# Two attention and feed-forward layers on one core: a planner that keeps one queue of DMA transfers, and an order worked out anew

## The chip, the core and the metric

The kernel runs on one core of a Trainium2 chip. Five engines of the core follow their own instruction streams and meet through semaphores: PE (matrix products), ACT (ScalarE: exp, gelu, copies), DVE (VectorE: element-wise work, transposes of 32x32 blocks, statistics), POOL (GpSimd: masks, small powers) and SP, which here does nothing but issue DMA transfers, in order.

The metric is the device time of one execution in microseconds (us), as the median of several runs. Before the change it is 542.36 us (three runs, 541.82 to 544.45).

## What is computed

The input x has 2048 rows of 512 numbers (bf16). Two layers are applied, both with the same weights, and each layer is an attention block followed by a gated feed-forward block, both added to x:

```python
x = A_x
x = x + _A_ref(_layernorm(x), A_wq, A_wk, A_wv, A_wo, A_beta)
x = x + _B_ref(_layernorm(x), B_w_gate, B_w_up, B_w_down)
x = x + _A_ref(_layernorm(x), A_wq, A_wk, A_wv, A_wo, A_beta)
x = x + _B_ref(_layernorm(x), B_w_gate, B_w_up, B_w_down)

def _B_ref(x, w_gate, w_up, w_down):          # 512 -> 1792 -> 512
    return _gelu(x @ w_gate) * (x @ w_up) @ w_down

# _A_ref, per segment s of 512 rows, 32 heads of 16 numbers:
logits = einsum('bhqd,bhkd->bhqk', qs, ks) * scale + mask     # causal inside the segment
a_dot = softmax(logits) @ vs
pq = phi(qs)                                                  # phi(t) = t+1 if t > 0 else exp(t)
a_mem = (pq @ M) / (pq @ z + 1e-06)                           # memory of the segments before
o = g * a_mem + (1 - g) * a_dot
M = M + phi(ks)^T @ vs ;  z = z + sum(phi(ks))
```

A segment reads the memory that the earlier segments of its layer left, so the attention of segments 0 to 3 is a chain, while the scores of a segment, its projections and the feed-forward blocks depend only on their own rows.

## The kernel before

The work is cut into eight pieces k = 0 to 7: segment k % 4 of layer k // 4. For each k there is an attention part (class `Att`) and a feed-forward part (class `Ffn`). All of x, all weights and all intermediate results stay in on-chip memory; the weights are loaded once at the start, in pieces, in between the first work.

**One attention part.** The rows are normalised (`Norm`): DVE takes the statistics of each block of 128 rows (`bn_stats`, `bn_aggr`), POOL makes the factor (`scales`: `ve`, then `rs` by a power), DVE writes the normalised rows `xn` (`normed`, L738), and a transpose brings them into `xnT`: by a DMA transpose issued from SP (`turn_later`, L627), or by PE for those named in `BY_PE`. PE makes the projections q, k, v; each product is copied out of the accumulator banks (`evict`, L661 on DVE or L662 on ACT, whichever comes first in the plan). The scores of a step are made by 16- or 32-row matmuls that run side by side (a "visit", L1452), ACT takes exp of up to four banks in one instruction (`pt`, L1524, 128x2048), POOL zeroes what lies above the diagonal (L1497), and PE multiplies with the values (a "flush", L1148, which reads `vaug` and `vS`). DVE turns and divides the result (`byq`, `r`, `ab`, `aT`). For the memory, ACT and DVE make phi of the keys in a tile `e`, SP issues its transpose into `phik`, and PE sums it with the values (`upd_item`). The odd heads' keys go to `kB` and part of the values to `vS` by small DMAs.

**One feed-forward part.** After the output projection (`wo`) and the addition to x (L1249 on DVE) the rows are normalised again; 14 products with `wg_sb` (gate), 14 with `wu_sb` (up), and 4 with `wd_sb` (down, 14 matmuls each). Of the gate products the first `RAW` (8) are copied out as they are by DVE or ACT and get their gelu later in place (`gel<-gel`); the others get it straight from the accumulator bank (`gel<-big`, L1304). exp and gelu use different tables, so ACT reloads a table on each change between the two.

**PE's three ways of tiling.** A product runs as one matmul of 128x128 weights (L670) or as four of 128x32 weights side by side (L679), as `BY_COLUMNS` says by the number of the visit; both stream the same number of columns. Scores use tiles of 16 or 32 rows.

**What sets the order.** Nothing is scheduled at run time and nothing by hand: when the program is built, a planner (class `Clocks`, `Engine`, `Slots` and the loop at the end of the function) runs the kernel on clocks of its own. Each engine has a list of jobs with a cost in us and a slack; each PE item has a due time (`DUE`, `BIAS`, `DUE_STEP`), and numbers that change every 8 us of planned time (`CHANGES`). Whatever the planner takes next is emitted next, so its costs and due times fix the order of the instructions on all five engines, SP's too. Where no item is ready, the scores are not done and a bank is free, the planner emits a product that nobody reads (`warm`), here called a filler.

The planner's notion of DMA is coarse. A weight piece of `kb` KB pushes one clock, `ck.dma`; a transposed tile is taken to be there a fixed time after its issue, plus a margin (`MARGIN` 1.0, `PHI_MARGIN` 1.7), or 1.2 us after the weights queued so far; `kB` and `vS` are taken to be there 2.0 us after their issue plus `KB_MARGIN` 1.5:

```python
def dma_load(self, t, kb):
    self.dma = max(self.dma, t + 1.1) + kb / 200.0

def told(t2):                                             # in turn_later
    t3 = max(t2 + 1.4 + margin, ck.dma + 1.2)
    ck.at(t3 - 0.2, lambda: landed(t3))
```

Those clocks exist only in the planner. On the chip each consumer waits on the semaphore of its own transfer.

## Time and profile before

| what | value |
|---|---|
| median of three runs | 542.36 us (541.82 to 544.45) |
| the profiled execution | 542.17 us, of which the trace covers a span of 540.4 us |
| instructions in the trace | 20717 |
| PE busy | 524.6 us, 97% of the span |
| DVE busy | 434.4 us, 80% |
| ACT busy | 419.1 us, 78% |
| POOL busy | 239.3 us, 44% |
| granted PE clock | 1.00 throughout |
| DMA moved | 29.66 MB, mean 55 GB/s |

How to read it: the profile gives the busy time of each engine, cut into stretches of time (windows), groups of instructions by line, the waits (which engine sat idle, and what released it), a timeline, and for each kind of DMA the median time from issue to landing. A row such as "PE big L679 <- DMA phik<-e: 1.3, 2, 1.1" says that PE's instructions of line 679 that write `big` waited 1.3 us in total for transfers from `e` to `phik`, twice, the longest 1.1 us. PE's busy time counts overlapping matmuls once. `PEld` is the loading of weights into PE, which overlaps the matmuls.

### The profile page before, as it was taken

Reading aid. Unit: us, or ns where it says so; the run is one execution under the profiler, and the core shown is the slowest. Engines: PE = TensorE matmul, PEld = TensorE weight load, DVE = VectorE, ACT = ScalarE, POOL = GpSimd, SP = SyncE. Lnnn points to the kernel's source line nnn. Section 1 sums busy time; section 2 is a strip of 40 time slices with the busy share of each in tenths; the row PEclk is TensorE's granted clock in tenths of the full one; section 3 lists DMA queues with packets and bytes.
Section 4 is the critical chain, followed back from the end, with each engine's and each line's share of the span. In section 5 each row is a group of like instructions: output and inputs, shape, how many; then the busy total and the mean of one; then the engine's idle time right before and its main releaser. Section 6 shows DMA issues by size and latency. Waiting matters only on the chain.

```text
span 540.4 us, 20717 instructions
## 1 busy us (share of the span) xinstructions
PE 524.6 (97%) x9084; PEld 274.6 (51%) x9144; DVE 434.4 (80%) x844; ACT 419.1 (78%) x406; POOL 239.3 (44%) x417
## 2 busy tenths in 40 slices
PE   8989898999999999999999999999999999999997
PEld 4436464854445444444544444454444554445884
DVE  7997899999998998589985898788975979476162
ACT  6899887999999878988789778987879646972500
POOL 6558144664456355634383343833484343111000
PEclk9999999999999999999999999999999999999999
DMA  8628841304411321100342113313310043000001
GB/s 255 196 41 181 213 73 23 58 4 73 69 23 32 56 58 35 28 13 13 63 70 41 32 25 57 52 32 52 41 52 2 12 81 53 3 1 32 11 1 39
DMA packets 69483, 29.66 MB, mean 55 GB/s; under 512 B 55120, under 2 KB 68944, under 8 KB 69392
## 3 DMA queue, kind: packets, MB, share of 16 engines
q1 hardware_dynamic: 69248, 28.32, 25.8%
q8 instruction: 71, 1.16, 0.9%
q14 instruction: 20, 0.16, 0.1%
q10 hardware_dynamic: 144, 0.01, 0.0%
HBM read 9.71 MB, written 2.10 MB: 22 GB/s over the span
## 4 chain that ended last, share of the span: by engine, by line
PE 87%; DVE 6%; issue 3%; ACT 2%; DMA 2%; POOL 0%; SPq 0%; DVEq 0%; POOLq 0%; ACTq 0%
PE big L670 42%; PE big L679 29%; PE big L1452 8%; PE big L1148 6%; ACT pt L1524 1%; DMA phik<-e 1%; DVE x_sb L1249 1%; DVE st L702 1%; DVE byq L1176 1%; DMA x_sb<-in_A_x_dram 1%; DVE xn L738 0%; DVE ab L1184 0%; DVE aT L1191 0%; PE big L768 0%; ACT lost L1541 0%
## 5 line engine op out<-in xcount | busy, mean ns | idle before, releaser
L1524 ACT ACTIVATE pt<-big 128x2048 bf16<-128x2048 f32 (+1 forms) x151 | 272.8, 1811 | 71.2 <-PE big L1452 58.5
L1497 POOL TENSOR_SCALAR_AFFINE_SELECT pt<-pt 64x256 bf16<-64x256 bf16 (+3 forms) x300 | 155.7, 545 | 233.3 <-ACT pt L1524 232.2
L1339 DVE TENSOR_TENSOR gel<-gel,big 128x512 bf16<-128x512 bf16 x112 | 74.8, 681 | 35.6 <-PE big L670 22.2
L670 PE MATMUL big<-xnT,wg_sb 128*128 128x256 bf16 (+1 forms) x389 | 66.7, 321 | 1.2 <-issue 1.0
L1249 DVE TENSOR_TENSOR x_sb<-x_sb,big 128x512 bf16<-128x512 bf16 (+1 forms) x65 | 43.0, 668 | 20.8 <-PE big L670 14.6
L1176 DVE STREAM_TRANSPOSE byq<-big 128x512 f32<-128x512 f32 x64 | 44.9, 702 | 17.4 <-PE big L1148 9.2
L670 PE MATMUL big<-xnT,wu_sb 128*128 128x256 bf16 (+1 forms) x347 | 54.7, 311 | 0.8 <-issue 0.6
L670 PE MATMUL big<-wd_sb,gel 128*128 128x512 bf16 (+2 forms) x240 | 54.0, 367 | 1.4 <-issue 1.0
L670 PEld LDWEIGHTS <-wg_sb 128*128 128x128 bf16 x399 | 37.5, 98 | 24.2 <-issue 3.0
L679 PE MATMUL big<-wd_sb,gel 128*32 128x512 bf16 x824 | 49.3, 380 | 0.1
L679 PE MATMUL big<-xnT,wu_sb 128*32 128x512 bf16 x812 | 47.6, 379 | 0.0
L1148 PE MATMUL big<-pt,vaug 128*32 128x64 bf16 (+5 forms) x1152 | 44.7, 263 | 2.0 <-ACT pt L1524 1.8
L670 PEld LDWEIGHTS <-wu_sb 128*128 128x128 bf16 x357 | 33.9, 98 | 18.1 <-issue 1.9
L702 DVE BATCH_NORM_STATS2 st<-x_sb 128x6 f32<-128x512 bf16 x60 | 40.7, 678 | 0.3
L1304 ACT ACTIVATE gel<-big 128x512 bf16<-128x512 f32 x58 | 32.3, 603 | 8.1 <-PE big L670 8.0
L679 PE MATMUL big<-xnT,wg_sb 128*32 128x512 bf16 (+1 forms) x644 | 37.0, 372 | 0.0
L670 PEld LDWEIGHTS <-gel 128*128 128x128 bf16 x256 | 23.2, 98 | 26.0 <-issue 2.5
L1304 ACT ACTIVATE gel<-gel 128x512 bf16<-128x512 bf16 x54 | 31.0, 656 | 0.0
L679 PEld LDWEIGHTS <-wu_sb 128*32 128x32 bf16 x812 | 21.2, 97 | 19.1 <-issue 1.7
L679 PEld LDWEIGHTS <-gel 128*32 128x32 bf16 x824 | 21.0, 97 | 19.3 <-issue 2.0
L738 DVE TENSOR_SCALAR xn<-x_sb,mv,rs 128x512 bf16<-128x512 bf16 x62 | 27.9, 493 | 2.8 <-POOL rs L725 2.6
L843 POOL TENSOR_SCALAR kS<-kf,maskA 128x256 bf16<-128x256 bf16 x28 | 29.3, 1047 | 0.8
(124 smaller groups left out, 799.4 us busy)
## 6 DMA issues: line engine op xcount, KB each, us to landing
out_dram<-x_sb SPq DMA_DIRECT2D x15, 128.0 KB, 1.7
vS<-vaug SPq DMA_DIRECT2D x14, 136.0 KB, 2.7
wg_sb<-in_B_w_gate_dram SPq DMA_DIRECT2D x8, 224.0 KB, 5.4
kB<-kf SPq DMA_DIRECT2D x28, 64.0 KB, 2.5
wu_sb<-in_B_w_up_dram SPq DMA_DIRECT2D x8, 224.0 KB, 4.8
wd_sb<-in_B_w_down_dram SPq DMA_DIRECT2D x7, 256.0 KB, 6.3
x_sb<-in_A_x_dram SPq DMA_DIRECT2D x3, 512.0 KB, 6.1
xnT<-xn SPq DMA_TRANSPOSE x48, 2.5
```

What stands on the lines that cost most here:

```text
L670: nc.tensor.matmul(out, lhsT=lhsT, rhs=rhs, start=start, stop=stop)
L679: nc.tensor.matmul(out[r], lhsT=lhsT[:, r], rhs=rhs[c], start=start, stop=stop, tile_position=(0, 32 * c))
L702: nc.vector.bn_stats(out=self.st6[:, 0, :], in_=x_sb[:, self.tt0 + j, :])
L843: eng.tensor_scalar(out=kS[:, b, t, :, u], in0=self.kf[:, b, :].rearrange("p (t h c) -> p t h c", h=2, c=Q)[:, t, 0, :], scalar1=(maskA, m ...
L1148: nc.tensor.matmul(ps()[32 * j:32 * j + 32, q0 + shift:q1 + shift], lhsT=va[:, ki, values_of(va, b, p, j)], rhs=step["pt"][:, j, c0:c0 + q ...
L1176: nc.vector.transpose(out=self.byq[:, c], in_=ps()[:])
L1249: ck.dve.post(ck.made(), slack, (0.683 - 0.00104 * (D - width), lambda: nc.vector.tensor_tensor(out=xt, in0=xt, in1=ps()[:, 0:width], op=A ...
L1304: return lambda: nc.scalar.activation(out=out(), in_=in_(), func=ACT.Gelu_apprx_tanh)
L1339: ck.dve.post(ck.made(), NORMAL, (0.683, lambda: nc.vector.tensor_tensor(out=hidden(g, h), in0=hidden(g, h), in1=banked(ps), op=ALU.mult), ...
L1452: nc.tensor.matmul(big[:, got[j], c0:c0 + q1 - q0], lhsT=lhsT, rhs=a.q[rows, b, q0:q1], start=True, stop=True, tile_position=(32 * j, 0))
L1497: nc.gpsimd.affine_select(out=v, in_=v, pattern=[[0, m], [by, size]], compare_op=ALU.is_ge, fill=0.0, base=by - 1, channel_multiplier=-1)
L1524: 0.172 + 0.000832 * width * len(banks_of), lambda g=g, st=st: nc.scalar.activation(out=pt[:, g, 0:width], in_=st, func=ACT.Exp, scale=SCA ...
```

## The change

The two programs compute the same, with the same tiles. Changed are the planner's costs and all its fitted numbers, and with them the order of all instructions. By parts:

1. **One queue of transfers.** `ck.transfer(t, lag, service)` keeps one clock for all DMA: a transfer starts when it was issued plus its lag, or when the one before it ended, and holds the queue for its service time. Weight pieces take 1.55 us lag and kb/350 us, a transposed tile 0.05 and 1.2 us (after an issue of 1.3 us), a piece of `kB` 1.4 and 0.5 us, a piece of `vS` 1.55 and 0.5 us.
2. **Margins.** `MARGIN` 1.0 to 0.4, `PHI_MARGIN` 1.7 to 0.5, `KB_MARGIN` 1.5 to 0.4, `LANDING` 1.5 to 0.4, the extra time for `amT` 1.0 to 0.4.
3. **Costs of some engine jobs**: phi on ACT 1.06 to 0.93 and 0.632 to 0.55, its DVE part 0.775 to 0.70, the copies to `kS` on POOL 1.05 to 0.96, a change of PE's tiling 0.108 to 0.097.
4. **The first norm of segment 1 by halves**: its factors are made for two blocks of rows at a time (`cuts`), so POOL has two pairs of small instructions in place of one, and the first two blocks of rows need not await the statistics of the last two. Its statistics are posted from 12.0 us of planned time in steps of 0.3, in place of 12.9 and 0.5.
5. **All fitted numbers new**: due times, `BIAS`, `BY_COLUMNS` and 63 rows of `CHANGES` (`TUNING` stays); `RAW` 8 to 12 and `RAW_FIRST` 3 to 1.

```diff
-RAW_FIRST = 3
-HALF_DUE = 0.8949
+RAW_FIRST = 1
+HALF_DUE = 1.8596
...
-LANDING = 1.5
+LANDING = 0.4
 GELU_TILES = 1
-RAW = 8
...
+RAW = 12
...
-MARGIN = 1.0
-PHI_MARGIN = 1.7
-KB_MARGIN = 1.5
...
+MARGIN = 0.4
+PHI_MARGIN = 0.5
+KB_MARGIN = 0.4
...
-    **{("qk", k): d for k, d in {0: 0.2818, 1: 0.6658, 2: 3.2809, 3: 6.5204, 4: -2.3807, 5: -1.4922, 6: -0.9853, 7: -0.256}.items()},
...
+    **{("qk", k): d for k, d in {0: -0.5076, 1: 0.8217, 2: 1.6258, 3: 6.026, 4: -0.6428, 5: 0.7702, 6: 3.6216, 7: 1.9024}.items()},
...
-        self.dma, self.seen = 0.0, -1
+        self.dma, self.heavy, self.seen = 0.0, 0.0, -1
...
     def dma_load(self, t, kb):
 
-        self.dma = max(self.dma, t + 1.1) + kb / 200.0
+        self.heavy = self.transfer(t, 1.55, kb / 350.0)
+
+    def transfer(self, t, lag, service):
+
+        self.dma = max(self.dma, t + lag) + service
+        return self.dma
...
+    def arrives(t, landed):
+        ck.at(t - 0.2, lambda: landed(t))
+
     def turn_later(t, slack, out, in_, landed, margin=0.0):
 
         def told(t2):
-            t3 = max(t2 + 1.4 + margin, ck.dma + 1.2)
+            t3 = ck.transfer(t2, 0.05, 1.2) + margin
             ck.at(t3 - 0.2, lambda: landed(t3))
...
-            self.mv, self.rs, self.xnT, self.n, self.left = None, None, None, [0] * parts, [TPS // parts] * parts
+            self.cuts = 2 if key == ("xnTa", 1) else parts
+            self.mv, self.rs, self.xnT, self.n, self.left = None, None, None, [0] * self.cuts, [TPS // parts] * parts
...
-                part = j * self.parts // TPS
+                part = j * self.cuts // TPS
                 self.n[part] += 1
-                if self.n[part] == TPS // self.parts:
+                if self.n[part] == TPS // self.cuts:
                     self.scales(part, t)
...
-                        ck.sp.post(max(t, ck.pe), tn.KB_SLACK, (0.55, lambda r=r: nc.sync.dma_start(
-                            out=self.kB[r], in_=self.kf[r]), lambda t2: ck.at(t2 + 1.8, lambda: landed(t2 + 2.0))))
+                        ck.sp.post(max(t, ck.pe), tn.KB_SLACK, (0.62, lambda r=r: nc.sync.dma_start(
+                            out=self.kB[r], in_=self.kf[r]), lambda t2: arrives(ck.transfer(t2, 1.4, 0.5) + KB_MARGIN, landed)))
...
-            ck.act.post(max(ready, ck.pe), slack, (1.06, exp, lambda t: ck.dve.post(
+            ck.act.post(max(ready, ck.pe), slack, (0.93, exp, lambda t: ck.dve.post(
...
-    norm_of_input(1, 12.9, 0.5)
+    norm_of_input(1, 12.0, 0.3)
```

By kind, the built programs differ only in a few counts. PE has 9144 matmuls before and 9270 after. Of these, 96 and 84 are `warm` products (19 whole ones at the very start in both; then 19 groups of four and 1 whole one before, 12 groups of four and 17 whole ones after); the other differences come from products that run as one matmul or as four. PE changes its way of tiling 305 times before and 304 times after. On ACT 25 fewer gelus come from a 128x512 bank and 24 more are done in place, and the table loads are 18 in both; DVE has 25 more copies of 128x512 gate products. SP issues the same 198 transfers.

In the instruction order, names are the program's tiles, followed by the shape written; "x3" stands for three in a row.

SP's stream from its second pair of `phik` transposes (memory of segment 0) to the last weight piece; `wu_sb` and `wd_sb` are weights, `x_sb` is the load of rows of x. Before:

```order
L627 DMA_TRANSPOSE xnT<-xn 128x4x128
L515 DMA wu_sb<-in_B_w_up_dram 128x896
L515 DMA x_sb<-in_A_x_dram 128x4x512
L515 DMA wu_sb<-in_B_w_up_dram 128x896
L627 DMA_TRANSPOSE phik<-e 128x4x128 x2
L515 DMA wu_sb<-in_B_w_up_dram 128x896
L515 DMA wd_sb<-in_B_w_down_dram 128x2x512
```

And in the change:

```order
L635 DMA_TRANSPOSE phik<-e 128x4x128
L520 DMA wu_sb<-in_B_w_up_dram 128x896 x3
L520 DMA wd_sb<-in_B_w_down_dram 128x2x512
L520 DMA wu_sb<-in_B_w_up_dram 128x896 x5
L880 DMA kB_131<-kf 16x2048
L635 DMA_TRANSPOSE phik<-e 128x4x128
L880 DMA kB_131<-kf 16x2048 x3
L635 DMA_TRANSPOSE phik<-e 128x4x128 x2
```

The load of the last segment's rows of x no longer stands ahead of the transposes (it comes later), the weights come in one block, and the last two `phik` transposes of segment 0 stand behind that block and behind pieces of `kB`.

ACT's stream at the first exps (`vaug` are copies of v products, `e` is phi of keys). Before:

```order
L662 ACTIVATE vaug_132<-big 128x16x2x16 x2
L1524 ACTIVATE pt<-big 128x2048
L662 ACTIVATE vaug_132<-big 128x16x2x16 x2
L1524 ACTIVATE pt<-big 128x2048 x3
L973 ACTIVATE e<-kf 128x512 x2
L1524 ACTIVATE pt<-big 128x2048
```

And in the change:

```order
L670 ACTIVATE vaug_132<-big 128x16x2x16 x2
L1534 ACTIVATE pt<-big 128x2048
L670 ACTIVATE vaug_132<-big 128x16x2x16 x2
L1534 ACTIVATE pt<-big 128x2048
L983 ACTIVATE e<-kf 128x512
L1534 ACTIVATE pt<-big 128x2048
L670 ACTIVATE q<-big 128x512
```

Three exps stood in a row; now one `e` and then copies of q and k products stand between them. On PE, in the same place, the two visits that followed each other directly are apart, with 1 filler and 10 products of q and k between them, and 2 more products ahead of the flush that followed the visits at once before.

DVE's stream at the gate products of the fourth piece (k = 3). Before:

```order
L1176 STREAM_TRANSPOSE byq<-big 128x512
L738 TENSOR_SCALAR xn<-x_sb,mv,rs 128x512 x3
L1031 TENSOR_TENSOR am<-big,rdm 128x512
L661 CAST gel<-big 128x512
L984 TENSOR_SCALAR e<-e 128x512
```

And in the change:

```order
L669 CAST gel<-big 128x512 x2
L1186 STREAM_TRANSPOSE byq<-big 128x512
L669 CAST gel<-big 128x512 x7
L1186 STREAM_TRANSPOSE byq<-big 128x512
L1190 RECIPROCAL r<-byq 128x32
L1194 TENSOR_TENSOR ab<-byq,r 128x2x16x16
L1201 STREAM_TRANSPOSE aT<-ab 128x512
L669 CAST gel<-big 128x512
```

DVE copied 1 gate product there and now copies 10.

183 lines of the change are left out of this document (92 added, 91 removed).

## The prediction

> **What bounds the kernel now.** First the page's busy times, then its chain of work that ended last.
>
> ```profile
> span 540.4 us, 20717 instructions
> PE 524.6 (97%) x9084; PEld 274.6 (51%) x9144; DVE 434.4 (80%) x844; ACT 419.1 (78%) x406; POOL 239.3 (44%) x417
> PE 87%; DVE 6%; issue 3%; ACT 2%; DMA 2%; POOL 0%; SPq 0%; DVEq 0%; POOLq 0%; ACTq 0%
> ```
>
> PE is busy for 97% of the span and is 87% of the chain. A new order of the same products can gain two things only: PE's idle time and the products nobody reads. Where PE idles is in the windows (span of the window, then busy us and instructions of PE, PEld, DVE, ACT, POOL, the clock, and DMA):
>
> ```profile
> 20.00:40.00 20.00, 17.61 (x301) 8.31 (x302) 19.30 (x45) 19.34 (x20) 12.18 (x18) 1.00 0.28 55
> 40.00:60.00 20.00, 18.30 (x332) 11.88 (x334) 14.62 (x33) 18.57 (x22) 12.18 (x23) 1.00 0.89 193
> 60.00:80.00 20.00, 19.85 (x290) 11.79 (x293) 19.32 (x41) 18.16 (x17) 7.24 (x15) 1.00 0.53 119
> 80.00:100.00 20.00, 18.60 (x442) 10.64 (x436) 19.59 (x36) 15.29 (x10) 9.18 (x18) 1.00 0.28 38
> 100.00:540.00 440.00, 431.77 (x7623) 223.54 (x7664) 345.26 (x650) 333.91 (x321) 187.77 (x320) 1.00 0.20 36
> ```
>
> From 20 to 100 us PE idles 2.39 + 1.70 + 0.15 + 1.40 = 5.64 us; in all of the 440 us behind, 8.23 us, which is 0.37 per 20 us and spread thin. The waits of PE, for 20 to 100 us and then for 100 to 540 us, name the causes (total, times, longest):
>
> ```profile
> PE big L1148 <- ACT pt L1524: 1.8, 1, 1.8
> PE big L679 <- DMA phik<-e: 1.3, 2, 1.1
> PE big L1148 <- DVE x_sb L1249: 1.1, 1, 1.1
> PE big L670 <- issue: 0.3, 2, 0.2
> PE big L1452 <- ACT pt L1524: 0.3, 1, 0.3
> ...
> PE big L670 <- issue: 4.1, 26, 0.2
> PE big L670 <- DVE r L1180: 0.2, 1, 0.2
> ```
>
> Three causes, 1.8 + 0.3 for exps, 1.3 for the last transposes of the first memory update, 1.1 for an addition to x, make 4.5 of the 5.64 us. Behind 100 us PE waits for no other engine longer than 0.2 us at a time. So the old order is almost perfect there, and the change is decided in the first 100 us: between 4.5 and 5.6 us can be had there, and nothing behind it.
>
> **Fillers: a known loss.** The timeline (start, duration, instruction; in brackets idle before it and its releaser) shows a filler's price:
>
> ```profile
> 23.49 0.52 PE L1148 MATMUL big<-pt,vaug 128*32 128x256 bf16 x16
> 23.83 2.19 PE L679 MATMUL big<-warm 128*32 128x512 bf16 x36
> 25.96 0.29 PE L1452 MATMUL big<-q,kf 16*128 16x256 bf16 x4
> 26.19 0.39 PE L1452 MATMUL big<-q,kf 16*128 16x256 bf16 x8
> 28.40 0.51 PE L1148 MATMUL big<-pt,vaug 128*32 128x256 bf16 x16 [1.82 <-ACT pt L1524]
> ```
>
> 36 matmuls are 9 groups of four, and from their start to the next visit pass 2.13 us: 0.237 us each, a change of tiling included. Without the tail it is (2.19 - 0.38) / 8 = 0.226, 0.38 being one matmul's whole duration in the group below. I take 0.23. Behind the 19 of the start the order holds 20 fillers before and 29 after: 9 more, +2.1 us (2.0 to 2.1). They lie on PE, so nothing hides them.
>
> ```profile
> L679 PE MATMUL big<-warm 128*32 128x512 bf16 x76 | 4.9, 379 | 0.0
> ```
>
> The Trainium skill (TensorE: Matmul & The Clock Gate, Back-to-back issue gap) gives about 131 ns for each product of 512 columns in a sustained stream; by that page nine fillers would cost 1.2 us. The trace has 0.23 and decides.
>
> **The same products, otherwise.** More products of 256 columns run as four matmuls, 305 changes of tiling become 304, and there are 126 more matmuls by number but no more columns to stream, fillers aside. The price of a whole and of a fourfold product, from the groups with few records missing:
>
> ```profile
> L670 PE MATMUL big<-wd_sb,gel 128*128 128x512 bf16 x212 | 50.9, 379 | 1.4 <-issue 1.0
> L679 PE MATMUL big<-wd_sb,gel 128*32 128x512 bf16 x824 | 49.3, 380 | 0.1
> ```
>
> 50.9 / 212 = 0.240 and 49.3 / 206 = 0.239 us. I cost both edits at 0; a change of tiling more or less is bounded by the 0.2 to 0.4 us of one visit, either sign.
>
> **The exp wait (2.1 us).** In the timeline above two visits follow each other at 25.96 and 26.19, and the flush behind them waits 1.82 us, until 28.40, for the exp of the first. The new order puts 10 products and a filler between the visits and 2 more products before the flush, 13 x 0.23 = 3.0 us on PE, more than the wait. ACT has as many copies ahead of that exp as before, so the wait goes; bounds 0 to 2.1 gained, I take all. The halved norm of segment 1 helps these products to stand there. POOL's factor for four and for two blocks of rows:
>
> ```profile
> L725 POOL TENSOR_TENSOR rs<-ve,mhalf 128x4 f32<-128x4 f32 x13 | 13.5, 1041 | 1.1
> L719 POOL TENSOR_SCALAR ve<-mv 128x4 f32<-128x4 f32 x13 | 3.0, 230 | 7.3 <-DVE mv L711 6.5 <-POOL pt L1497 0.2
> L725 POOL TENSOR_TENSOR rs<-ve,mhalf 128x2 f32<-128x2 f32 x4 | 2.9, 715 | 0.3
> ```
>
> The first two blocks have theirs after 0.23 + 0.72 = 0.95 us in place of 1.27, and need not await the last two statistics. The second pair is 0.63 us more on POOL, 2 x 0.95 - 1.27, beside the 7.8 us that POOL idles in 20 to 40 us; without that cover it would be 0.6 us.
>
> **The phik wait (1.3 us).** Of the transposes of `phik`, first all in the run, then those between 48 and 60 us; and DVE's two steps of a half phi of q:
>
> ```profile
> DMA to landing us min/median/max: 2.4/2.4/7.2
> ...
> L627 SPq DMA_TRANSPOSE phik<-e x2: 1202/1263/1324, 49.7 to 51.0; - x2
> DMA to landing us min/median/max: 6.2/6.7/7.2
> ...
> L957 DVE SCALAR_TENSOR_TENSOR phiq<-q,phiq 128x1024 bf16<-128x1024 bf16 x12 | 16.9, 1411 | 0.4
> L953 DVE TENSOR_SCALAR phiq<-phiq 128x1024 bf16<-128x1024 bf16 x12 | 5.9, 493 | 1.6 <-ACT phiq L950 1.6
> ```
>
> These two took 6.2 and 7.2 us in place of 2.4, since weights and rows of x were queued ahead of them. The old planner did not know, the new one does. But the last two transposes now stand behind nine weight pieces and pieces of `kB`, and the `e` of the last has on DVE two such phi of q ahead of it, 2 x (0.49 + 1.41) = 3.8 us, that came later before. What was late by the queue is then late by DVE. Bounds: 0 to 1.3 us left; I leave 0.7.
>
> **The wait for x (1.1 us).** A flush finds its bank only when DVE has added an earlier one to x; DVE is busy 19.59 of 20 us there. The new order makes DVE's work in that stretch no less. Bounds 0 to 1.1; I leave 0.4.
>
> **Smaller margins.** Medians from issue to landing, and the planner's own sums:
>
> ```profile
> vS<-vaug SPq DMA_DIRECT2D x14, 136.0 KB, 2.7
> kB<-kf SPq DMA_DIRECT2D x28, 64.0 KB, 2.5
> xnT<-xn SPq DMA_TRANSPOSE x48, 2.5
> ```
>
> For `xnT` the planner allowed 1.3 + 1.4 + 1.0 = 3.7 us from the start of the issue and now 1.3 + 0.05 + 1.2 + 0.4 = 2.95; for `phik` 4.4 and 3.05; for `kB` 4.05 and 2.92; for `vS` 4.05 and 3.15. All still lie 0.4 to 0.65 us above the median, so a lone transfer isn't late. What is new is small slips where a chain runs later than planned: 0 to 1.5 us, I take 0.4.
>
> **Gate copies on DVE.** By shape:
>
> ```profile
> L661 DVE CAST gel<-big 128x512 bf16<-128x512 f32 x31 | 21.1, 685 | 4.4 <-PE big L670 2.2 <-PE big L679 1.7 <-PE big L1452 0.2
> L1304 ACT ACTIVATE gel<-big 128x512 bf16<-128x512 f32 x58 | 32.3, 603 | 8.1 <-PE big L670 8.0
> L1304 ACT ACTIVATE gel<-gel 128x512 bf16<-128x512 bf16 x54 | 31.0, 656 | 0.0
> ```
>
> 25 more copies at 0.685 are +17.1 us on DVE; on ACT 25 x 0.603 leave and 24 x 0.656 come, +0.7. DVE's 434.4 become 451.5, 84% of the span: hidden behind PE on average, but not everywhere (below). On the path I take 0.
>
> **Sum.** Stalls removed: 5.1 (between 4.5 and 5.6), less what is left or new, 0.7 + 0.4 + 0.4 = 1.5, is 3.6. Against the profiled execution's 542.17 us: 542.17 + 2.1 - 3.6 = 540.7. That execution stands 0.2 below the median of 542.36, so I forecast 540.9 us, 0.27% faster. About 0.5%, 2.7 us, is what a measurement of this kernel can tell from no change; the forecast lies inside.
>
> **Rivals.**
>
> *All stalls go.* If the one queue is right in every place, 542.36 + 2.1 - 5.6 = 538.9. For it: the three waits are what a coarse DMA clock and a coarse start would miss. Against it: DVE, busy 96% and more of 20 to 40 and of 60 to 100 us, has to keep up with a PE that runs earlier.
>
> *The waits move only.* The last `e` and the addition to x are as late as before, and only the exp wait goes: 542.36 + 2.1 - 2.1 = 542.4. The change would then have repaired in its plan what the chip has for another reason.
>
> *DVE becomes the bound.* From 60 to 200 us:
>
> ```profile
> 60.00:200.00 140.00, 136.60 (x2717) 74.49 (x2732) 131.89 (x256) 123.96 (x113) 71.89 (x118) 1.00 0.29 54
> DVE gel L1339 <- PE big L679: 1.8, 1, 1.8
> DVE x_sb L1249 <- PE big L679: 1.2, 2, 0.7
> ```
>
> DVE has 8.1 us left of 140, and its two longest waits are 1.8 and 1.2 us. The second and third gate blocks fall there; the order gives them 17 copies on DVE where 9 stood, 8 x 0.685 = 5.5 us. If DVE can't take more than half of that in its gaps, PE waits for free banks for 2.8 us, and the early gain is lost at the same engine but for the exp: 542.36 + 2.1 - 2.1 + 2.8 = 545.2. It decides once DVE's work up to 200 us grows by more than about 3 us, its two waits. Against it: what DVE does for other parts may move out of the stretch, and banks let PE run ahead. The Trainium skill (TensorEngine Tiling (Array Packing), PSUM Bottleneck) warns that when PE is made faster the copying out of banks may be the limit, and to use both ScalarE and VectorE for it; the change shifts copies towards VectorE, and the trace's 131.89 of 140 says that the warning is near.
>
> *Margins too small.* At each of the six boundaries between pieces behind 100 us a transposed row comes late by the 0.75 us that `xnT` lost: 6 x 0.75 = 4.5 and 542.36 - 1.5 + 4.5 = 545.4. For it: nothing there waits now, so there is only loss to have. Against it: medians below the plan in all four kinds.
>
> **How the numbers follow.** Forecast 0.42, all stalls gone 0.24, waits move 0.19, DVE the bound 0.09, margins 0.06. Faster by over 0.5% (below 539.65) are all stalls gone and 0.04 of the forecast's lower edge, 0.28; slower (above 545.07) are the last two but for 0.02 that stay just under, 0.13; within, 0.59. The forecast's own range is 539.4 to 542.4 (stalls left 0 to 3.0). The range for 8 in 10 reaches from 537.9, the 538.9 of all stalls gone less 1.0 of the thin idle, to 545.0, just under the two slower cases.
>
> **What would show it.** PE's idle time in 20 to 100 us falls from 5.64 to about 2 us, and PE's rows of `warm` rise by 9 products. No wait of a flush for `pt` over 0.5 us before 40 us. Transposes of `phik` in 45 to 60 us land in 2.4 to 4 us. DVE's busy time rises to about 451 us; if PE waits for DVE between 100 and 200 us by more than 1 us in total, the DVE rival holds. Idle of PE behind 100 us above 10 us in place of 8.23 would prove the margins. The forecast is wrong if early idle stays above 4 us or falls below 0.5.

## The result: slower by 0.9%

| | median | runs |
|---|---|---|
| before | 542.36 us | 541.82 to 544.45 |
| after | 547.90 us | 546.94 to 548.98 |

The ratio is 1.0093, with a 95% interval of 1.0068 to 1.0118. The forecast was 540.9 us; the range ended at 545.0. The profiled execution of the changed kernel took 548.07 us with a span of 546.3, which is 5.9 more than the 540.4 of before. That execution has a mean granted clock of 0.997 (3.4 us at half speed lower the mean of such a span by 0.003); the other four of the changed kernel have 1.000 and are as long, 546.94 to 548.98 us, so what its trace shows of a slow clock is not what they lost.

The page of the changed kernel, its span, busy times and the shares of the chain that ended last:

```profile
span 546.3 us, 21016 instructions
PE 528.2 (97%) x9210; PEld 276.7 (51%) x9270; DVE 446.7 (82%) x869; ACT 416.8 (76%) x402; POOL 238.5 (44%) x423
PE 74%; DVE 12%; ACT 6%; DMA 3%; issue 3%; SPq 1%; POOL 0%; ACTq 0%; DVEq 0%
```

PE is busy 97% again, but only 74% of the chain lies on it, 87% before. The windows of the same stretches (columns as before):

```profile
20.00:40.00 20.00, 19.09 (x342) 8.91 (x341) 18.76 (x47) 19.52 (x21) 11.10 (x20) 1.00 0.55 113
40.00:60.00 20.00, 16.98 (x277) 11.46 (x274) 15.43 (x34) 19.07 (x21) 13.97 (x20) 1.00 0.72 180
60.00:80.00 20.00, 19.58 (x449) 13.02 (x452) 15.79 (x34) 14.14 (x15) 3.88 (x10) 0.91 0.27 62
80.00:100.00 20.00, 19.49 (x454) 11.16 (x458) 18.74 (x44) 19.22 (x22) 11.76 (x26) 1.00 0.30 56
100.00:540.00 440.00, 431.25 (x7537) 221.62 (x7577) 360.24 (x671) 331.32 (x307) 185.38 (x320) 1.00 0.20 36
```

PE idles 0.91 us from 20 to 40 us in place of 2.39, but 3.02 from 40 to 60 in place of 1.70, and from 60 to 80 us the granted clock is 0.91. PE's waits, first from 20 to 100 us, then from 100 us on:

```profile
PE big L687 <- DMA phik<-e: 2.2, 1, 2.2
PE big L1462 <- ACT pt L1534: 1.7, 3, 0.9
PE big L678 <- issue: 0.3, 2, 0.2
...
PE big L678 <- issue: 3.5, 22, 0.2
PE big L1462 <- ACT pt L1534: 1.0, 2, 0.5
PE big L687 <- issue: 0.6, 1, 0.6
PE big L1462 <- issue: 0.5, 1, 0.5
PE big L687 <- DMA xnT<-xn: 0.4, 1, 0.4
```

The long exp wait of a flush (1.8 us) and the wait for x (1.1) are gone, as forecast. The wait for `phik` has grown from 1.3 to 2.2, and waits for exps, for `xnT` and for nothing named have come behind 100 us.

**A ledger.** Busy and idle time do not tell the loss, since the products nobody reads (fillers below) count as busy, and a slow clock too. So I summed, from PE's weight loads in the trace, the time beyond what the needed products take when the clock is granted in full: 0.216 us for 512 columns, start to start, plus the median of a change of tiling (0.32 us for a visit, 0.11 for the others). What is left is lost: fillers, idle time, half clock. In us, up to a point of the span, and the same for the plan's own clock:

| lost up to | 20 | 30 | 50 | 65 | 100 | 115 | 540 us |
|---|---|---|---|---|---|---|---|
| before, on the chip | 7.4 | 13.3 | 13.9 | 15.5 | 17.0 | 17.1 | 18.4 |
| before, in its plan | 7.1 | | 14.4 | 14.4 | 15.4 | 15.5 | 18.5 |
| after, on the chip | 7.5 | 10.6 | 14.1 | 17.8 | 18.6 | 21.1 | 24.2 |
| after, in its plan | 7.1 | | 13.9 | 13.9 | 14.0 | 16.4 | 16.2 |

The last column explains the result for the two profiled executions: 24.2 - 18.4 = 5.8 of the 5.9 us. The old plan foresaw its loss to 0.1 us (its clock ends at 537.4, and PE's last weight load in the trace starts at 537.3), but in part by luck: at 115 us the chip was 1.6 us behind it, and behind 115 us it lost 1.3 us where the plan has 3.0. The new plan promised 2.1 us less (its clock ends at 535.3) and the chip lost 8 us more than it promised. At 30 us the new order is 2.7 us ahead; at 50 us nothing is left of it, neither on the chip nor in the plan. Then come three losses: 50 to 65 us, 100 to 115 us (this one planned), and behind 115 us. Each is tried below.

**What the plan's promise consists of.** The new planner counts a change of PE's tiling at 0.097 us in place of 0.108: 305 x 0.108 = 32.9 us before, 304 x 0.097 = 29.5 after. That is 3.4 us less for almost the same changes, more than the whole promise of 2.1; at the old cost the same order would end at 538.7 in its plan (535.3 + 304 x 0.011), behind the old one. The trace does not bear the lower cost out: a visit with its two changes takes 0.32 + 0.11 = 0.43 us in it, and the planners count 0.226 for a visit of the smallest kind and two changes, 0.44 before and 0.42 after. This is also why the row of the new plan falls from 16.4 to 16.2 us behind 115 us, which a loss that is only added to can't do. Held against the same prices, the new plan holds no gain on PE.

### The profile page after: what moved, and what is told of

Read it like the earlier page. It is cut to its first block, busy times and chain, and to the rows that moved or that the text cites. A ratio compares the mean times of both kernels' runs of the same rounds, so it can differ in the third digit from the quotient of the medians.

```text
span 546.3 us, 21016 instructions
## 1 busy us (share of the span) xinstructions
PE 528.2 (97%) x9210; PEld 276.7 (51%) x9270; DVE 446.7 (82%) x869; ACT 416.8 (76%) x402; POOL 238.5 (44%) x423
## 3 DMA queue, kind: packets, MB, share of 16 engines
q8 instruction: 72, 1.18, 0.9%
## 4 chain that ended last, share of the span: by engine, by line
PE 74%; DVE 12%; ACT 6%; DMA 3%; issue 3%; SPq 1%; POOL 0%; ACTq 0%; DVEq 0%
PE big L678 36%; PE big L687 25%; PE big L1462 7%; PE big L1158 6%; ACT pt L1534 3%; DVE gel L1349 1%; DVE st L711 1%; DMA xnT<-xn 1%; DVE phiq L967 1%; DVE byq L1186 1%; DMA phik<-e 1%; DVE gel L669 1%; DVE xn L747 1%; DMA wu_sb<-in_B_w_up_dram 1%; SPq L520 1%
## 5 line engine op out<-in xcount | busy, mean ns | idle before, releaser
L1507 POOL TENSOR_SCALAR_AFFINE_SELECT pt<-pt 64x256 bf16<-64x256 bf16 (+4 forms) x304 | 151.2, 524 | 237.5 <-ACT pt L1534 222.6
L678 PE MATMUL big<-xnT,wg_sb 128*128 128x512 bf16 (+1 forms) x366 | 66.1, 329 | 1.6 <-issue 0.6
L687 PE MATMUL big<-xnT,wu_sb 128*32 128x512 bf16 (+1 forms) x1100 | 56.9, 358 | 0.0
L1186 DVE STREAM_TRANSPOSE byq<-big 128x512 f32<-128x512 f32 x64 | 45.1, 706 | 10.6 <-PE big L1158 10.1
L678 PE MATMUL big<-xnT,wu_sb 128*128 128x256 bf16 (+1 forms) x276 | 47.3, 320 | 1.1 <-issue 0.6
L669 DVE CAST gel<-big 128x512 bf16<-128x512 f32 x54 | 36.3, 683 | 10.6 <-PE big L678 5.2
L687 PEld LDWEIGHTS <-wu_sb 128*32 128x32 bf16 x1100 | 30.4, 99 | 20.6 <-issue 1.7
L1314 ACT ACTIVATE gel<-gel 128x512 bf16<-128x512 bf16 x74 | 39.7, 623 | 0.0
L678 PEld LDWEIGHTS <-wu_sb 128*128 128x128 bf16 x285 | 26.8, 98 | 17.1 <-issue 1.9
L852 POOL TENSOR_SCALAR kS<-kf,maskB 128x256 bf16<-128x256 bf16 x28 | 30.5, 1090 | 0.4
L1462 PE MATMUL big<-q,kf 16*128 16x64 bf16 (+5 forms) x576 | 27.7, 263 | 2.0 <-ACT pt L1534 1.8
```

What stands on the lines that cost most here:

```text
L669: ck.dve.post(ck.made(), slack, (cost, lambda: nc.vector.tensor_copy(out=dst(), in_=src()), end), taken=taken)
L678: nc.tensor.matmul(out, lhsT=lhsT, rhs=rhs, start=start, stop=stop)
L687: nc.tensor.matmul(out[r], lhsT=lhsT[:, r], rhs=rhs[c], start=start, stop=stop, tile_position=(0, 32 * c))
L852: eng.tensor_scalar(out=kS[:, b, t, :, u], in0=self.kf[:, b, :].rearrange("p (t h c) -> p t h c", h=2, c=Q)[:, t, 0, :], scalar1=(maskA, m ...
L1186: nc.vector.transpose(out=self.byq[:, c], in_=ps()[:])
L1462: nc.tensor.matmul(big[:, got[j], c0:c0 + q1 - q0], lhsT=lhsT, rhs=a.q[rows, b, q0:q1], start=True, stop=True, tile_position=(32 * j, 0))
```

## Experiments

In all kernels but those named as planned anew, the edit is made where instructions are issued, with the planner's clocks untouched, so that all other instructions keep their order. Ratios are to the kernel before.

### 1. Without the fillers

```diff
-                product(ps()[:], warm[:], wide)
+                (only the planner's counters, as product() moves them)
                 ck.unread(Clocks.MM[512])
```

The changed kernel without its 29, the kernel before without its 20:

> The changed kernel without the 29 products that nobody reads, their places in the plan kept, so every other instruction stands in the same order. If they lie on PE, as I costed them, the time falls by 29 x 0.216 = 6.3 us, from 547.9 to 541.6. If they only fill time in which PE would wait for banks and exps anyway, idle time takes their place and the time stays between 546.5 and 548.

> The kernel before without its 20 products that nobody reads, all else in the same order. On PE: 20 x 0.216 = 4.3 us less, 538.1. Only filling waits: 541.5 to 542.5. The difference between this fall and that of the changed kernel is what the 9 additional ones cost: 2.0 us by the first theory, 0 by the second.

Measured: the kernel before 543.02 us, ratio 1.0001 (0.9993 to 1.0010): no gain. The changed kernel 544.36, 1.0040 (1.0024 to 1.0056): 3.5 us less than the 547.9 with them. For the kernel before without fillers, PE's waits from 20 to 100 us, and then two rows of PE's timeline:

```profile
PE big L1452 <- ACT pt L1524: 3.1, 3, 1.9
PE big L1148 <- ACT pt L1524: 1.8, 1, 1.8
```

```profile
25.75 0.29 PE L1452 MATMUL big<-q,kf 16*128 16x256 bf16 x4 [1.93 <-ACT pt L1524]
28.18 0.83 PE L1148 MATMUL big<-pt,vaug 128*32 128x256 bf16 x16 [1.81 <-ACT pt L1524]
```

Where nine fillers stood, PE now waits 1.93 us for the same exp, and the visit starts at 25.75 in place of 25.96. The windows of the same run show what is worse:

```profile
26.00:34.00 8.00, 6.18 (x85) 2.34 (x77) 6.30 (x17) 7.54 (x7) 4.76 (x7) 0.57 0.13 27
```

After two idle stretches of 1.93 and 1.81 us the clock stands at half for most of 8 us. So in the kernel before the fillers cost nothing: they stand where PE would wait, and they keep the clock up. For the changed kernel the time alone does not say so, since it fell by 3.5 us, of the 6.3 that the fillers would cost on PE. By the ledger both orders have lost about the same at 50 us with fillers (13.9 and 14.1) and without (15.1 and 15.1). So up to there the fillers are not what is lost, and the 3.5 us come later. In the two profiled executions PE comes 1.3 us later to the `phik` products and the transpose is there, so the wait and the half clock of experiment 2 don't happen (3.2 us gained from 55 to 65 us), and three stalls of 0.5 to 0.6 us between 250 and 310 us are gone, for a reason that I did not find.

### 2. The wait for phik

SP's timeline of the changed kernel, and PE's:

```profile
49.68 1.45 SPq L880 DMA_DIRECT2D kB<-kf  x1
51.23 2.46 SPq L635 DMA_TRANSPOSE phik<-e  x1
53.76 1.84 SPq L880 DMA_DIRECT2D kB<-kf  x3
55.70 1.23 SPq L635 DMA_TRANSPOSE phik<-e  x1
...
57.77 0.24 PE L687 MATMUL big<-vaug,phik 128*32 128x32 bf16 x12
60.20 0.60 PE L687 MATMUL big<-vaug,phik 128*32 128x32 bf16 x52 [2.18 <-DMA phik<-e]
60.61 2.75 PE L687 MATMUL big<-xnT,wu_sb 128*32 128x256 bf16 x48
```

and DVE's, for the `e` of the last transpose:

```profile
53.06 0.76 DVE L986 SCALAR_TENSOR_TENSOR e<-kf,e 128x512 bf16<-128x512 bf16 x1
```

The `e` is done at 53.8; the plan had it at 54.4. DVE is early, not late. But SP, behind nine weight pieces and a slow transpose (2.46 us to issue), begins three pieces of `kB` only at 53.76, where the plan had finished them at 53.2. The transpose goes out at 55.70 and lands 4.45 us later. The plan had it issued from 54.4 on and there at 57.0, and at 57.5 with its margin: of the 3.1 us that it lands late, 1.3 are SP's and 1.9 the longer way from issue to landing. The second price is in the windows behind the wait:

```profile
60.00:61.00 1.00, 0.80 (x61) 0.74 (x64) 0.06 (x1) 0.23 (x1) 0.00 (x0) 0.61 0.00 0
61.00:62.00 1.00, 1.00 (x26) 0.85 (x20) 0.63 (x1) 0.00 (x0) 0.00 (x0) 0.50 0.00 0
62.00:63.00 1.00, 1.00 (x28) 0.74 (x20) 0.38 (x1) 0.00 (x0) 0.00 (x0) 0.50 0.06 16
63.00:64.00 1.00, 1.00 (x26) 0.55 (x19) 0.62 (x3) 0.04 (x1) 0.00 (x0) 0.68 0.00 0
```

PE's clock is granted at half for 3.4 us: the 48 matmuls at 60.61 take 2.75 us, and 1.50 in the next kernel. Two edits take the transpose out of the queue, in the changed kernel and, the first, in the kernel before:

```diff
 a_wu_early, b_wu_early: the eight loads of wu issued together
+  ahead of the first piece of wd (26 us) in the changed kernel,
+  ahead of the first transpose of phik (27 us) in the kernel before
 a_kb_act: the four pieces of kB of segment 1
-  nc.sync.dma_start(out=self.kB[r], in_=self.kf[r])
+  nc.scalar.dma_start(out=self.kB[r], in_=self.kf[r])
```

> The changed kernel with its eight pieces of wu issued at about 26 us, where SP is idle, in place of 45 to 50 us; nothing else moves. If the weight pieces ahead of them on SP and in the DMA engines make the last transpose of phik late, it is issued at about 53.8 (its e is ready then) in place of 55.7 and lands by 58.2: PE's wait of 2.2 us goes, and with it the half clock behind it, about 1.4 us: 544.3. If DVE sets it, as I predicted (e late), or if another thing is late next, the idle at 58 us only shrinks by some tenths: 547 to 547.9.

> The changed kernel with the four pieces of kB of segment 1 issued by ACT in place of SP. If SP's order is what makes the last phik transpose late (three pieces of kB, 1.84 us, stand between its e and its issue), it goes out at 53.8 and the wait and the half clock go: 544.5. If the transfers themselves are slow (weights in the DMA engines), the landing stays near 60 and the time at 547.5 to 548; if ACT's four issues delay its exps, 548 or more.

> The kernel before with its eight pieces of wu issued at about 27 us, where SP is idle until 35, in place of 45 to 57 us. In the changed kernel the same edit brought the last phik transposes in by 58.1 and let PE run 2.9 us earlier at 65 us, of which 1.1 were left at the end. Theory: here the 1.65 us that PE loses at 55 us go, and since the plan behind has its old margins nothing gives them back: 542.4 - 1.6 = 540.8, which beats both kernels. Rival: the gain is eaten by the next late thing (the addition to x at 92 us waits for DVE, which is not earlier): 542.0 to 542.5.

With `wu` early the changed kernel takes 546.72 us (1.0069, 1.0054 to 1.0084). SP's timeline and PE's show the cure:

```profile
51.07 1.83 SPq L884 DMA_DIRECT2D kB<-kf  x3
54.10 1.20 SPq L639 DMA_TRANSPOSE phik<-e  x1
...
58.02 0.69 PE L691 MATMUL big<-vaug,phik 128*32 128x32 bf16 x64
```

The transpose now lands 2.4 us after its issue, all 64 matmuls run without a wait, and against the changed kernel, instruction by instruction, PE is 2.9 us earlier at 65 us. At the end 1.1 are left: 0.7 go between 100 and 120 us, 0.3 at 253, and 0.9 at 456 us in one wait for `xnT`. So what made this wait is shown: the queue of transfers ahead of the transpose. What it is worth in the median is not: the interval overlaps that of the changed kernel (1.0068 to 1.0118).

The wait also differs between executions whose instructions stand in the same order. In the two runs of experiment 3 on the changed kernel SP is not held at that place, though the same nine weight pieces stand ahead: the first piece of `kB` takes 0.60 us to issue and the transpose behind it 1.23 and 1.26, where the rows above have 1.45 and 2.46; without fillers, with both engines as they were, it is 0.60 and 1.22. So this slow issuing is of one execution, and why it came is not shown. The last transpose goes out earlier, and PE waits 1.0 us in the one with lighter gelus (`a_act_light`) and not at all in the one with lighter DVE (`a_dve_light`):

```profile
54.83 1.20 SPq L635 DMA_TRANSPOSE phik<-e  x1
58.98 0.56 PE L687 MATMUL big<-vaug,phik 128*32 128x32 bf16 x52 [1.00 <-DMA phik<-e]
...
53.85 1.22 SPq L635 DMA_TRANSPOSE phik<-e  x1
57.77 0.80 PE L687 MATMUL big<-vaug,phik 128*32 128x32 bf16 x64
```

Neither has a half clock there. By 65 us PE is 2.6 and 3.2 us earlier than in the changed kernel, instruction by instruction; yet the medians of these runs are 547.1. So the 3.7 us from 50 to 65 us are the loss of one execution; with the clock of the other four at 1.000, they lost at least a part of their time elsewhere, and where was not traced.

With `kB` issued by ACT, 548.64 us (1.0108, 1.0086 to 1.0131). The wait for `phik` goes, and PE waits 2.1 us for a gelu in its stead, as ACT, which issues the pieces in its own order, gets to it late.

In the kernel before, `wu` early gives 541.28 us, ratio 0.9986 (0.9975 to 0.9998): a little faster than both kernels. PE's waits from 20 to 100 us:

```profile
PE big L1152 <- ACT pt L1528: 1.8, 1, 1.8
PE big L1152 <- DVE x_sb L1253: 1.1, 1, 1.1
PE big L1456 <- ACT pt L1528: 0.3, 1, 0.3
```

The `phik` wait is gone, the others stand, and of 1.6 us gained at 60 us 1.4 are there at the end.

### 3. Is DVE or ACT late?

```diff
 a_dve_light, b_dve_light: gate times up, on DVE, half the columns
-  out=hidden(g, h), in0=hidden(g, h), in1=banked(ps)
+  out=half(hidden(g, h)), in0=half(hidden(g, h)), in1=half(banked(ps))
 a_act_light: second pass of the gelu, on ACT, half the columns
```

> The changed kernel with each of its gate-times-up products on DVE done on half its columns (the output is then not the reference's); same order. DVE has some 112 x 0.3 = 34 us less to do. If DVE, 17 us busier than before, is what makes PE late behind 60 us, most of the 2.5 us of new waits behind 100 us go and some of the early ones: 543.5 to 545.5. If the waits are for transfers and exps that the plan took as too early, DVE's work does not matter: 546.5 to 548.

> The same edit in the kernel before, as the control. It has one long wait for DVE (1.1 us for x at 92 us) and about 1 us of thin ones: 540.8 to 542.2 by either theory.

> The changed kernel with the second pass of the gelu on ACT done on half its columns (the output is then not the reference's); same order. ACT has some 78 x 0.2 = 16 us less to do. If late exps make PE late (visits wait 2.7 us for pt in all, 1.0 of it behind 100 us), the time falls by 1 to 2.5: 545.5 to 547. If not, 547.5 to 548.

Measured: 547.06 us (1.0087, 1.0069 to 1.0104), 542.48 (1.0002, 0.9989 to 1.0015) and 547.08 (1.0085, 1.0067 to 1.0103). DVE is busy 26 us less than in the changed kernel (420.4 us; 408.1 in the control), ACT 15 us less (401.6). Neither engine's load moves the time by more than the noise. From 100 to 150 us, where the changed kernel loses 3.0 us by the ledger, the runs with the lighter engines are as late, instruction by instruction, to 0.2 us: it is the plan itself, which puts six fillers at 112 us, and two waits of 0.5 and 0.6 us stand beside them.

The wait for `xnT` varies too from one execution to the next. PE's waits in the run with lighter gelus, from 100 us on:

```profile
PE big L678 <- DMA xnT<-xn: 2.1, 2, 1.2
PE big L1462 <- ACT pt L1534: 0.9, 2, 0.5
PE big L687 <- issue: 0.8, 1, 0.8
PE big L687 <- DMA xnT<-xn: 0.4, 1, 0.4
```

In six executions of the new order these waits for `xnT` come to 0.6, 1.5, 2.0, 1.1, 2.5 and, without fillers, 0 us; in four of the old order to 0.

### 4. Margin, or fit?

Four orders planned anew, to be held against their own plan's clock:

```diff
 m_new_large: the changed kernel with MARGIN 1.0, PHI_MARGIN 1.7, KB_MARGIN 1.5, LANDING 1.5
 m_new_uncut: the changed kernel with
-            self.cuts = 2 if key == ("xnTa", 1) else parts
+            self.cuts = parts
 m_old_large: the new model with all numbers of the kernel before
 m_old_small: m_old_large with MARGIN 0.4, PHI_MARGIN 0.5, KB_MARGIN 0.4, LANDING 0.4
```

> The changed kernel with the old margins (MARGIN 1.0, PHI_MARGIN 1.7, KB_MARGIN 1.5, LANDING 1.5), its model of the queue and its fitted numbers kept. The planner makes another order, whose own clock ends at 555.4 us, since the numbers were fitted to the small margins; the test is how far the time lies above the plan's clock. The kernel before: 542.4 against 537.4, 5.0 above. The changed one: 547.9 against 535.3, 12.6 above. If the small margins make it late, this one lies 5 to 7 above, 560.5 to 562.5. If the new model's other costs are too low (exps, kS, tiling), 9 to 13 above, 564.5 to 568.

> The changed kernel with the first norm of segment 1 scaled in one piece as before; small margins and fitted numbers kept. Another order again, whose own clock ends at 552.2. It shows whether the small margins do the same harm in an order that was not fitted to them. Margins: 9 to 13 above, 561 to 565. If only the fitted order is late, because the fit sought out just what the model has too early, 5 to 7 above, 557 to 559.

> The new planner (one queue with its durations, new costs, halved norm) with all numbers of the kernel before, margins too. Its own clock ends at 548.9. By the margins 5 to 7 above, 554 to 556; if the new costs are too low, 8 or more above, 557 and more.

> As m_old_large, but with the four small margins. Its own clock ends at 561.2. By the margins 9 to 13 above, 570 to 574; if only the fitted order is late, 5 to 7 above, 566 to 568.

| | margins | time | plan's clock | above it |
|---|---|---|---|---|
| before | large | 542.4 | 537.4 | 5.0 |
| after | small | 547.9 | 535.3 | 12.6 |
| m_new_large | large | 562.4 | 555.4 | 7.0 |
| m_new_uncut | small | 557.4 | 552.2 | 5.2 |
| m_old_large | large | 558.2 | 548.9 | 9.3 |
| m_old_small | small | 569.6 | 561.2 | 8.4 |

The margins don't order the last column: 5.2 and 8.4 with small ones, 7.0 and 9.3 with large ones. The row of before can't be compared with the others directly, since all five others are counted with the cheaper changes of tiling, which alone is some 3.4 us. Of these five the changed order keeps its plan worst. That would fit an order that was picked, among many, because its plan looked best, but it is not shown. These orders also have 9 to 23 us more lost time than the changed one, so that a late transfer can fall where PE waits anyway. One thing does follow the margins: PE waits for `xnT` behind 100 us in both orders with small ones (0.8 and 3.6 us) and in none with large ones. And each of them shows how narrow a fit is: one part undone costs 9 us and more as long as nothing is fitted again, so a part's worth can't be read from such a run.

### 5. Does ACT set the pace from 20 to 50 us?

```diff
+  part = 3 * width // 4 if ck.pe < 50.0 else width
-  nc.scalar.activation(out=pt[:, g, 0:width], in_=st, ...)
+  nc.scalar.activation(out=pt[:, g, 0:part], in_=st, ...)
+  nc.gpsimd.memset(pt[:, g, part:width], 1.0)
```

in both kernels without fillers.

> The kernel before without its unread products, and up to 50 us of the plan each of the 14 exps of scores does three quarters of its columns on ACT; the last quarter is filled with ones by POOL (so the output is not the reference's). ACT has 14 x 0.43 = 6 us less to do by 50 us. Without the unread products alone PE lost 7.9 us between 20 and 50 us and the time stayed at 543.0. If ACT, busy 29 of these 30 us, sets the pace there, 3 to 5 of the 7.9 go: 538 to 540. If DVE (94% busy) or the way from product to exp to flush sets it, at most 1 goes: 542 to 543.

> The same in the changed kernel, which without its unread products lost 7.8 us between 20 and 50 us and took 544.4. ACT the pace: 539.5 to 541.5. Not ACT: 543.5 to 544.5. If both orders lose the same there with and without the lighter exps, the new order has nothing to gain on PE in this stretch, whatever wait it removes.

542.90 us (1.0012, 1.0000 to 1.0023) and 544.13 (1.0035, 1.0022 to 1.0049): nothing. ACT's busy time from 20 to 50 us falls from 28.0 to 24.4 us and from 28.7 to 24.4, and PE waits less for exps; but from 18 to 50 us in the changed order

```profile
PE big L678 <- DMA xnT<-xn: 2.8, 1, 2.8
PE big L1462 <- ACT pt L1535: 1.5, 1, 1.5
```

the next limit stands right behind, the transposed rows of segment 2 (at 44 us, ahead of its q products). My theory that ACT alone sets the pace falls. What the runs show is that neither fixed order loses less than 13.9 us by 50 us, with fillers, without them, or with lighter exps; which of the limits behind each other sets that was not taken apart further.

### 6. How much room has a late transpose?

```diff
+  a small load on SP ahead of the last (late1) or the last two (late2) transposes
+  of xn in each group from segment 2 on: load(spare[:, j - 2], xv[:, 0, 0:64])
```

> The kernel before with one small load of 16 KB on SP ahead of the last of the four transposes of xn, in each group from segment 2 on (11 groups): about 0.5 us on SP, so the last row comes about 0.5 us later. The old plan allowed 1.0 us above its own sum for these and PE never waits for xnT behind 100 us: 542.4 to 543.0.

> The same with two such loads, ahead of the third and the fourth transpose: the last row comes about 1.0 us later, which uses up the old margin: 542.5 to 545.

> The changed kernel with one such load in each group. If the small margin is what costs it time behind 100 us (PE waits 0.4 to 2.5 us for xnT there in five executions), it has no room left: each group that was already late pays the 0.5 us in full, half of the 11 or more: 550 to 553. If those waits are chance hits of single transfers and the margin still holds in most groups, 547.5 to 548.5.

> The changed kernel with two such loads in each group, 1.0 us later. Margin the cause: 553 to 558, and its loss over its own time is at least 3 us more than that of the kernel before with the same loads. Chance hits: 548 to 550, a loss like that of the kernel before.

| | one load | two loads |
|---|---|---|
| before | 546.52, 1.0066 (1.0040 to 1.0092) | 549.70, 1.0121 (1.0089 to 1.0153) |
| after | 552.14, 1.0165 (1.0126 to 1.0203) | 552.88, 1.0186 (1.0143 to 1.0229) |

The old order loses 4.2 us with one load, the changed one 4.2; with two loads 7.3 and 5.0. My expectation for the old one, none to 0.6, was wrong, and with it the theory that the old margin keeps room for a late transpose. By what I had expected of two loads, at least 3 us more for the changed order if the margin is the cause, the margin is not the cause. Two of the old order's eleven groups pay, 4.1 us at 138 us and 1.0 at 215; in the changed order five do (both against the profiled executions without loads), 0.4 to 3.5 us each. SP's and PE's timeline of the kernel before with one load:

```profile
135.87 0.58 SPq L515 DMA_DIRECT2D spare<-in_A_x_dram  x1
136.56 1.22 SPq L628 DMA_TRANSPOSE xnT<-xn  x1
...
140.71 1.04 PE L680 MATMUL big<-xnT,wq_sb 128*32 128x512 bf16 x8 [2.50 <-DVE byq L1179]
```

Without the load, the last transpose of this group was issued at 135.0 and landed 2.4 us later, just in time; now it lands 4.1 us after its issue, at 140.7, and that is what PE waits for (the `byq` that is named was done long before). Behind the wait the clock is at half again:

```profile
140.00:142.00 2.00, 1.29 (x16) 0.58 (x20) 0.70 (x2) 0.00 (x0) 1.68 (x4) 0.58 0.36 70
142.00:144.00 2.00, 2.00 (x28) 0.60 (x20) 0.00 (x0) 0.60 (x1) 0.00 (x0) 0.57 0.38 76
```

So the dose was larger than the 0.5 us that I meant it to be, and in both orders a few places have no room at all. The new order has more of them in these traces; that its margins are why was not shown.

## Why the prediction was wrong

**What bounds the kernel: right, but read too simply.** PE is full and the early stalls can be had only where nothing else stands behind them. I took each wait as worth its length, and I wrote that the change is decided in the first 100 us and nothing can be had behind it. That sentence failed: of the 5.8 us, 1.6 are lost up to 100 us and 4.2 behind, since a new order can add stalls where the old one had none. The ledger shows that waits of one stretch are one loss in several shapes: idle time, a filler, a slow clock.

**Exp wait, "I take all" of 2.1: failed.** The wait went, for the reason given, and at 30 us the new order was 2.7 us ahead. By 50 us that was given back, as PE's timeline of the changed kernel shows:

```profile
43.71 1.90 PE L678 MATMUL big<-warm 128*128 128x512 bf16 x8
...
48.47 0.40 PE L1462 MATMUL big<-q,kf 16*128 16x256 bf16 x8 [0.89 <-ACT pt L1534]
...
112.21 1.46 PE L678 MATMUL big<-warm 128*128 128x512 bf16 x6
```

Eight fillers and a wait of a visit for its exp stand before 50 us (the third row belongs to the loss at 112 us). From 20 to 50 us 6.5 us are lost before and 6.6 after. The row that I quoted was a warning: DVE 19.30 and ACT 19.34 busy of 20 us in that window. But experiment 5 speaks against ACT alone. What the fillers at 43.71 stand for can be seen where they are left out (`a_nofill`): there PE waits 1.18 us, up to 45.62, for the last transposed rows of segment 2, which SP issues at 42 us in both. In the old order PE has other products at that time. Worth: 0 in place of 2.1.

**Fillers, "+2.1", "nothing hides them": failed.** Nine more there are; in the kernel before fillers cost nothing, and up to 50 us neither do they in the changed one (experiment 1). They are how the planner writes a wait. In the sum they and the exp wait cancel, which is what the rival in which the waits only move has (542.4), and up to 50 us it is right.

**The phik wait, "I leave 0.7": failed in the profiled execution.** It lost 3.7 us from 50 to 65 us in place of the 1.6 of before: +2.1 where I had a gain of 0.6. I named a late `e` on DVE; the `e` was early. Late were SP, by 1.3 us, with three pieces of `kB` ahead of the transpose, and then the landing, by 1.9. The pieces stood in the order, in the sentence "behind nine weight pieces and pieces of `kB`", and I did not add up their issue times. And I had no term for a slow clock behind an idle PE. In the traces with lighter DVE and ACT the wait is 0 and 1.0 us and the clock stays full, and four of the five executions of the changed kernel were as long without the slow clock, so this step does not explain the median.

**The wait for x, "I leave 0.4": right.** It is gone; 65 to 100 us lose 0.8 us in place of 1.5.

**Smaller margins, "I take 0.4": the size failed, the mechanism is open.** Behind 100 us the new order loses 5.6 us, the old one 1.4. Of the difference, 2.4 come from 100 to 115 us; this is the largest of the steps. The plan itself has it, and it had no term at all, since I asked only whether the old stalls went and not what new ones the plan had. 1.8 come behind 115 us: waits for `xnT` that differ from execution to execution, exps at visits (1.0), and waits without a name (1.1). The rival of too small margins gave 545.4; it had the right place and sign, but PE's idle time behind 100 us is 8.75 us, not the 10 that I had named as its proof, and experiments 4 and 6 do not show the margin to be the cause. What costs the 1.8 us stays open.

**Gate copies, 0 on the path: right.** DVE's busy time rose to 446.7 (forecast 451), and relieving it by 26 us gained nothing. The DVE rival falls. (Its row "1.2, 2, 0.7" I read as a wait of 1.2 us; it is two waits, the longer 0.7.)

**The signs.** PE's idle time from 20 to 100 us fell from 5.64 to 0.91 + 3.02 + 0.42 + 0.51 = 4.86 us, above the 4 that I had named as a sign of being wrong, and the two transposes of `phik` between 50 and 57 us landed after 5.1 and 4.5 us, not 2.4 to 4.

The sum by the ledger, for the profiled executions: +0.2 up to 50 us, +2.1, -0.7, +2.4, +1.8: 5.8 us, where I had 2.1 - 3.6 = -1.5. That sum also took 5.1 us of stalls as removable where the named causes come to 4.5; the 0.6 between them had no cause.

## What to carry to other kernels

Before a wait is counted as a gain, look at how full the other engines are in its window: here the wait that went, where ACT and DVE are busy 96%, came back within 20 us, as dummy products ahead of a transposed tile and as a wait for an exp. Where a transfer is late, add up what its issuing queue has ahead of it from the moment its source is ready; here moving eight weight loads to an idle stretch of that queue gave 0.14% (541.28 us; the interval only just excludes no change), and a newly fitted order of everything lost 0.9%. Do not compare two plans by their own clocks before both are counted at the same prices: here one lowered cost makes 3.4 us, more than the whole promise of 2.1. And set the kept plan (537.4 planned, 537.3 traced) above the promised one (535.3 planned, 543.2 traced): the best of many fitted plans may be best where its model is wrong. Last, profile more than one execution before a stall is taken for the cause of the median.

## What was not expected of the hardware

**Half clock after short idling.** PE's granted clock fell to 0.50 after 2.18 us of idle time in the changed kernel and after 2.50 us in experiment 6, each time for about 3.4 us, and after two idle stretches of 1.93 and 1.81 us close together for 7 us; after 1.82 us alone, in the kernel before, it stayed at 1.00. The Trainium skill (TensorE: Matmul & The Clock Gate, Part 1: The HAM clock gate (the "warmup" mystery)) has the half rate after an idle window of about 3.4 us and full rate after as long a busy one; the length of the slow stretch agrees, the idle time that brings it on is shorter here.

The length of the idle time alone does not decide. After 1.82 us the clock also fell, in `m_old_large` and `m_old_small`; after 2.07 us it stayed at 1.00 in `a_kb_act`; and in `b_late2` it fell where the longest idle time was 1.42 us. What orders these is a grid: in every kept trace with more than one half-clock stretch, their starts lie whole multiples of 3.413 us apart (60.23 and 548.33 us in the changed kernel, 143 steps), and the grid lies elsewhere in each execution. Between 12 and 535 us there are 18 such stretches in the kept traces, and in the step of the grid just ahead of each PE was busy for 24 to 55% of the time (1.23 of 3.41 us in the changed kernel). In `a_kb_act` (its grid counted back from the one half-clock stretch at its end) the 2.07 us lie across two steps, with 2.53 and 2.23 us busy. The share is not quite all: the step with 1.59 us in the kernel before was not followed by a half clock, one with 1.59 us in `m_old_large` was. So the same wait can bring the half clock on in one execution and not in the next: of 77 executions of the kernel before that stood beside the experiments, 23 have a mean granted clock of 0.994 to 0.997 and take 542.56 to 546.42 us, the others 0.999 or 1.000 and 541.20 to 543.04.

**A transpose directly behind a copy.** Alone, a DMA transpose of one tile lands 2.4 to 2.5 us after its issue. Issued right behind a small load in experiment 6 it took 3.3 to 4.4 us in six of ten cases and 2.4 to 2.6 in the others; behind the three pieces of `kB` 4.45 us, and 2.4 when the last of them had been issued 1.2 us earlier. The planner's queue, which lets a transfer start when the one before it has ended, foresaw less.
